# An RWKV-6 attention with an erf-softplus MLP on one Trainium2 core: the seven-product projection applied to four more units, with activations in chunks through PSUM

## The chip, the cores and the metric

The kernel runs on one core of a Trainium2 chip. Its engines are TensorE (PE, matrix products), VectorE (DVE), ScalarE (ACT), GpSimd (POOL) and SyncE (SP, here only a queue of DMAs). PSUM is the memory that the products are written to. The kernel's tiles in it are `pp0`, `pp1` and `y` of 1024 fp32 elements for each partition and two buffers `m` of 512, and no others.

The metric is the time of one execution in microseconds, and lower is better. A profile is one execution recorded by the hardware profiler, with the start and length of every instruction.

## The reference

All data are fp32. Attention has 4 batches, 8 heads, 768 tokens and head dimension 48. Its output, as 3072 rows of 384, goes through a two-layer MLP of width 2048.

```python
for t in range(S):
    cur = einsum('bhd,bhe->bhde', u * k[t], v[t])
    y[t] = einsum('bhd,bhde->bhe', r[t], state + cur)
    state = w[t][..., None] * state + einsum('bhd,bhe->bhde', k[t], v[t])
x = y as (3072, 384)
h = x @ w_in
sp = maximum(h, 0) + log1p(exp(-abs(h)))      # softplus
out = (h * erf(sp)) @ w_out
```

## The kernel before

**Units and steps.** The work is cut into 12 units (`n_steps`): a unit is 128 tokens of two batches, so 256 rows (`UNIT`) of the MLP. A unit passes through three stages. In step s the kernel attends unit s, computes the hidden layer of unit s-1 and projects unit s-3. All engines follow an order written out by hand: inside `tc.manual_schedule` (line 940) every engine executes its instructions in the order in which the program issues them, and dependencies through tiles become waits.

**Attention** works on chunks of 128 tokens. The masked products inside a chunk are built by levels: at level n, `level_products` (line 443) multiplies keys and queries that were decayed up to blocks of half that size, `take_level` (line 459) puts the result in `own`, and `scale` (line 257) multiplies keys and queries by the decay totals of that level (`tot_sb`, made on POOL at line 315). From step 4 on (`DIRECT`), the lowest levels are instead computed straight on DVE and POOL in `prepare` (lines 343 to 428): products of rows at distance 1 to 4 on DVE, 5 to 15 on POOL (lines 374 to 381), reduced on DVE into `sums` (line 367), sent through DRAM (`by_blocks`, `by_tokens`) and spread into `own` (line 423). `prepare(s + 1)` is a generator that step s advances with `next(following)`, so its parts lie among the step's other work.

**A late step** (`attend_late`, line 571, s > 4) issues in this order: `from_own` of the unit before (first group, into `y`), `fence` (a small DVE read of `y`), level five products, their scaling and masking, `from_own` (second group) and `through_state` of the unit before (lines 476 and 499), whose result ACT copies from `y` to `xT`. Then come the preparation of unit s+1, the scaling of `kT` by `spread` (line 595), and the places 0 to 4 at which MLP work is issued; between places 1 and 2 are level six, `spread_blocks`, the state product (`state_part`, line 530) and the sum `middle` (line 613), and between places 2 and 3 the new state (line 621). `products` (line 131) alternates between `pp0` and `pp1`.

**The MLP** comes in pieces: `piece` (line 893) advances a generator by one. A hidden piece (`hidden`, line 724) makes 512 elements for each partition in an `m` buffer, which ACT copies to `h`; eight pieces make a unit, in two tiles `h` of 8 by 256. After each tile `activate` queues three stages in `later`: softplus and Erf on ACT over the whole tile (2048 elements), and a multiplication on DVE in two halves. `advance` (line 875) issues these stages, up to one ACT activation at a time. Softplus and Erf each need an ACT table load, since they alternate.

**Projection.** Units 0 to 7 use `project` (line 767), eight pieces of four matmuls of 384 columns (each fp32 matmul is two instructions in the profile). Units 8 to 11 use `project_fast` (line 829): the matrices of activations and weights are cut into quarters and multiplied with seven quarter products in place of eight, after Winograd's form of Strassen's method. It needs four sums of weights (`mix_weights`, line 796, issued in steps 8 to 10) and four sums of activation quarters (`blend`, line 812, each 1024 elements), and two sums at the output (lines 864 and 868). `FAST = 8` is the first unit that uses it. The pieces of a step are ordered by strings in `in_order` (line 903), in which A is `advance`, P a projection piece and H a hidden piece.

Of the kernel before, what the change touches and what calls it, by code (L numbers as in the profile page):

```python
# [11 lines left out]
FP32 = mybir.dt.float32  # L12
I32 = mybir.dt.int32
# [4 lines left out]
P = 128  # L18
FAST = 8
EP = 64  # L20
HC = 64
# [40 lines left out]
def kernel(  # L62
# [34 lines left out]
    hid = ctx.enter_context(tc.tile_pool(name="hid", bufs=4))  # L97
    act = ctx.enter_context(tc.tile_pool(name="act", bufs=2))
    wide = ctx.enter_context(tc.tile_pool(name="wide", bufs=4))
# [25 lines left out]
    ND = DM // NJ  # L125
    mixed = const.tile([P, 3, FG, ND], FP32, name="mixed")
    y = ps_y.tile([P, NE, NJ, NP // 2, C], FP32, name="y")

# [138 lines left out]
    def prepare(s):  # L267
# [132 lines left out]
        for level in range(1, near_log(s)):  # L400
            scale(s, level)
        yield
        if near == NEAR:
# [15 lines left out]
        scale(s, near_log(s))  # L419
        if s > FAST:  # L420
            next(mixing)
        nb = HC // NEAR
# [6 lines left out]
        )  # L429
        if s == FAST + 3:  # L430
            next(mixing)

# [66 lines left out]
    def through_state(s, xT):  # L499

        c, in_t, _, _, S, _, _ = parts_of(s)
        for h, state in enumerate((S, middle)):
            if not (c or h):
                continue
            t = slice(h * HC, (h + 1) * HC)
            for j in range(NJ):
                for q in range(0, NP, 2):
                    for e in range(NE):
                        for p in (q + e, q + 1 - e):
                            n = j * NP + p  # L510
                            nc.tensor.matmul(  # L511
                                y[at(e, p), e, j, p // 2, t],
                                lhsT=state[rows(e), n, :], rhs=in_t[rows(e), 0, n, t],
                                start=False, stop=True, skip_group_check=True,
                            )

        y3 = att.tile([P, UNIT], FP32, name="y3", bufs=1)
        nc.scalar.copy(y3[:].rearrange("p (j t) -> p j t", j=NJ), y[:, 1, :, 1])
        for j in range(NJ):
            nc.scalar.copy(xT[:, 0:2, j * C : (j + 1) * C], y[:, 0, j])  # L520
        nc.scalar.copy(xT[:, 2, :].rearrange("p (j t) -> p j t", j=NJ), y[:, 1, :, 0])
        for kk in range(KT):
            n = D // KT
            for e, queue in enumerate((nc.sync, nc.scalar)):
                queue.dma_start(
                    out=xT[e * EP + D : (e + 1) * EP, kk, :],
                    in_=y3[e * EP + kk * n : e * EP + (kk + 1) * n, :],
                )
# [41 lines left out]

    def attend_late(s, place):

# [3 lines left out]
        if before:  # L576
            from_own(before, ready[before][0], 1)
            fence()
        pp = products([P, NE, JP, HC])
        level_products(pp, RK, LOG - 1)  # L580
# [10 lines left out]
        next(following, None)  # L591
        if s == FAST + 3:
            blend(FAST, gated[FAST])
        kT = kTs[s]
# [3 lines left out]
        )  # L598
        place(0)
        next(following, None)  # L600
        place(1)

        pp = products([P, NE, JP, HC])
        level_products(pp, RK, LOG)
        if s + 1 < n_steps:
            spread_blocks(s + 1, pp)
        take_level(own, pp, LOG)
        ps = products([P, NC, JP, HC])
        ps = [ps[:, h] for h in range(NC)]
        state_part(s, kT, ps)  # L610
        scale(s, LOG)
        for e in range(NE):
            nc.vector.tensor_add(middle[rows(e)], faded[0][rows(e)], ps[0][rows(e), :, :D])
        place(2)
        next(following, None)
        if s < n_steps - SPC:
# [3 lines left out]
            for e in range(NE):  # L620
                nc.vector.tensor_add(S_next[rows(e)], faded[1][rows(e)], ps[1][rows(e), :, :D])
        place(3)
        for _ in following:
            pass
        place(4)

# [94 lines left out]

    later = []

    def hidden(of, xT, gs, cut):


        def activate(h):
# [3 lines left out]
            def softplus():  # L731
                held.append(act.tile([P, FG, UNIT], FP32, name="sp"))
                nc.scalar.activation(held[0][:], h[:], AF.Softplus)  # L733

            def erf():
                nc.scalar.activation(held[0][:], held[0][:], AF.Erf)  # L736

# [4 lines left out]
            later.extend([(softplus, True), (erf, True), (multiply, False)])  # L742
            if of > FAST and len(gs) == NG:
                later.append((lambda: blend(of, gs), False))

        for g in range(NG):
            h = hid.tile([P, FG, UNIT], FP32, name="h")
            gs.append(h)
            for f in range(0, FG, FT):
# [12 lines left out]
                nc.scalar.copy(h[:, f : f + FT, :], ps[:])  # L762
                if f == FG - FT:
                    activate(h)
# [44 lines left out]

    blends = {}  # L810

    def blend(of, gs):

        if of % 2:
            rooms = [wide.tile([P, 2, DM, 2], I32, name="words", bufs=3) for _ in range(3)]
            rooms = [x[:].rearrange("p x n two -> p (x n two)").bitcast(FP32) for x in rooms]
        else:
            two = att.tile([P, 2, JP, C], FP32, name="rk1", bufs=1)
            one = ins.tile([P, JP, C], FP32, name="w")
            rooms = [x.rearrange("p n t -> p (n t)") for x in (two[:, 0], two[:, 1], one[:])]  # L820
        s1, s2, s4 = (x[:, : FG * C].rearrange("p (f t) -> p f t", t=C) for x in rooms)
        (a11, a21), (a12, a22) = [[g[:, :, j * C : (j + 1) * C] for j in range(NJ)] for g in gs]
        nc.vector.tensor_add(s1, a21, a22)
        nc.vector.tensor_sub(s2, s1, a11)
        nc.vector.tensor_sub(s4, a12, s2)
        nc.vector.tensor_sub(a21, a11, a21)
        blends[of] = s1, s2, a21, s4

# [74 lines left out]
    def in_order(s, k):  # L903


        order = ("APPPAPP", "APPP", "HH", "AHHH", "AHHH", "PPAPP")
        if s == DIRECT:
            order = ("APPP", "APPP", "APPHH", "AHHH", "AHHH")
        if s >= FAST + 3:
            order = ("PAPPPAP", "PAP", "HH", "AHHH", "AHHH", "PPPAP")  # L910
        for what in order[k]:
# [4 lines left out]
            else:  # L916
                piece(hids, s - 1)


    CONVERT = (  # L920
# [19 lines left out]
    with tc.manual_schedule(  # L940
# [20 lines left out]
        for s in range(n_steps):  # L961
# [8 lines left out]
            def place(n):  # L970
                if n == (LOG - 1 if s <= DIRECT else 2) and DIRECT - 1 <= s < n_steps - 2:
                    load_rows(s + 2)
                for due in {(3, 4): (5,), (4, 3): (6,), (4, 5): (7,)}.get((s, n), ()):
                    load_w(due)
                if s > DIRECT and n == 2 and s + 3 < n_steps:
                    load_w(s + 3)
                if s >= DIRECT:
# [13 lines left out]
                beside(s, next(places))  # L991

            if s > DIRECT:
                attend_late(s, place)
                continue
# [8 lines left out]
            if s + 2 < n_steps:  # L1004
                load_step(s + 2)
                if s + 2 == DIRECT:
                    load_rows(s + 2)
        s = n_steps - 1
        from_own(s, ready[s][0], 1)
        fence()  # L1010
        advance()
        piece(projs, s - 2)
        from_own(s, ready[s][0], 0)
        through_state(s, xTs[s])
        in_order(s + 1, 5)
        for k in range(1, 15):
            in_order(s + 1 + k // 5, k % 5)

# [95 lines left out]
```

## Time and profile before

| | us |
|---|---|
| median of 3 runs (607.51 to 608.27) | 607.88 |
| profiled execution | 607.66 |
| its span | 605.9 |
| PE busy | 592.9 |
| PE weight loads busy (beside PE) | 470.8 |
| DVE busy | 439.5 |
| ACT busy | 294.3 |
| POOL busy | 296.1 |

Steps 5 to 11 begin at 202.9, 247.4, 295.2, 341.5, 387.8, 434.05 and 480.85 us of the span, and what follows step 11 at 524.57. Busy time (us) in each of these stretches:

| step | length | PE | DVE | ACT | POOL |
|---|---|---|---|---|---|
| 5 | 44.50 | 44.50 | 38.85 | 20.20 | 31.88 |
| 6 | 47.80 | 46.54 | 38.92 | 20.80 | 33.55 |
| 7 | 46.30 | 46.30 | 38.93 | 20.79 | 32.00 |
| 8 | 46.30 | 46.30 | 40.67 | 20.80 | 32.19 |
| 9 | 46.25 | 46.25 | 40.64 | 20.79 | 33.39 |
| 10 | 46.80 | 46.58 | 41.17 | 20.79 | 26.55 |
| 11 | 43.72 | 43.72 | 20.02 | 20.82 | 0 |
| after | 81.33 | 77.80 | 22.39 | 31.94 | 0 |

A share of busy time alone does not say what a change is worth: an engine's waits, and the order in which its instructions stand, decide when its results come. The chain of the profile follows the work back from the last instruction, at each step to what released it. The granted clock of PE was full (1.00) in every one of these stretches.

### The profile page before, as it was taken

Reading aid. Unit: us, or ns where it says so; the run is one execution under the profiler, and the core shown is the slowest. Engines: PE = TensorE matmul, PEld = TensorE weight load, DVE = VectorE, ACT = ScalarE, POOL = GpSimd, SP = SyncE. Lnnn points to the kernel's source line nnn. Section 1 sums busy time; section 2 is a strip of 40 time slices with the busy share of each in tenths; the row PEclk is TensorE's granted clock in tenths of the full one; section 3 lists DMA queues with packets and bytes.
Section 4 is the critical chain, followed back from the end, with each engine's and each line's share of the span. In section 5 each row is a group of like instructions: output and inputs, shape, how many; then the busy total and the mean of one; then the engine's idle time right before and its main releaser. Section 6 shows DMA issues by size and latency. Waiting matters only on the chain.

```text
span 605.9 us, 16024 instructions
## 1 busy us (share of the span) xinstructions
PE 592.9 (98%) x7050; PEld 470.8 (78%) x7050; DVE 439.5 (73%) x487; ACT 294.3 (49%) x378; POOL 296.1 (49%) x295
## 2 busy tenths in 40 slices
PE   8889999999999999999999999999999999999997
PEld 7668787678668768658758858858857898898997
DVE  5688597895995897897697798898798756105141
ACT  2648887635536533442552462462462463652440
POOL 4349175602397489489369569659659200000000
PEclk9999999999999999999999999999999999999999
DMA  8376471441333405325325334334321300000000
GB/s 322 117 279 222 156 257 58 202 147 13 138 78 132 131 26 176 68 84 190 48 103 157 76 109 154 75 112 120 71 102 56 70 8 28 1 21 13 1 28 26
DMA packets 51373, 63.29 MB, mean 104 GB/s; under 512 B 34920, under 2 KB 40296, under 8 KB 49896
## 3 DMA queue, kind: packets, MB, share of 16 engines
q1 hardware_dynamic: 50152, 61.68, 32.0%
q8 instruction: 55, 0.90, 0.6%
q10 hardware_dynamic: 1152, 0.59, 0.4%
q14 instruction: 14, 0.11, 0.1%
HBM read 52.39 MB, written 8.69 MB: 101 GB/s over the span
## 4 chain that ended last, share of the span: by engine, by line
PE 85%; DVE 7%; issue 2%; POOL 2%; ACT 2%; DMA 1%; SPq 0%; DVEq 0%; POOLq 0%; ACTq 0%
PE m L753 38%; PE m L782 25%; PE m L844 12%; PE pp L451 5%; DVE in L263 2%; PE y L485 2%; PE y L511 1%; PE pp L537 1%; POOL w_in_sb L232 1%; DMA in<-in_rkw 1%; DVE w_in_sb L228 1%; PE pp L682 1%; DVE sums L367 1%; DVE pp L220 1%; DVE own L463 1%
## 5 line engine op out<-in xcount | busy, mean ns | idle before, releaser
L753 PE MATMUL m<-xT,w_in_sb 128*128 128x256 f32 x1152 | 257.3, 382 | 2.4 <-DVE w_in_sb L228 1.2
L753 PEld LDWEIGHTS m<-xT,w_in_sb 128*128 128x128 f32 x1152 | 216.1, 190 | 34.6 <-issue 3.6
L782 PE MATMUL m<-w_out_sb,h 128*128 128x384 f32 x512 | 168.6, 489 | 0.0
L782 PEld LDWEIGHTS m<-w_out_sb,h 128*128 128x128 f32 x512 | 96.2, 190 | 65.3
L762 ACT COPY h<-m 128x512 f32<-128x512 f32 x96 | 56.0, 583 | 132.1 <-PE m L753 131.9
L263 DVE TENSOR_TENSOR in<-in,tot_sb 128x1024 f32<-128x1024 f32 (+1 forms) x60 | 84.4, 1414 | 18.6 <-PE pp L451 16.8
L740 DVE TENSOR_TENSOR h<-h,sp 128x1024 f32<-128x1024 f32 x48 | 74.6, 1594 | 23.8 <-ACT sp L736 23.6
L381 POOL TENSOR_TENSOR words<-words,rest 128x528 f32<-128x528 f32 (+10 forms) x77 | 85.6, 1111 | 6.0
L377 POOL TENSOR_TENSOR rk<-words 128x528 f32<-128x528 f32 (+3 forms) x28 | 44.5, 1590 | 78.7 <-DVE sums L367 68.3
L315 POOL TENSOR_TENSOR tot_sb<-tot_sb 128x256 f32<-128x256 f32 (+4 forms) x60 | 57.6, 960 | 4.5
L451 PEld LDWEIGHTS pp<-in 48*64 48x64 f32 (+1 forms) x2368 | 33.8, 125 | 16.1 <-issue 8.3
L733 ACT ACTIVATE sp<-h 128x2048 f32<-128x2048 f32 x24 | 45.9, 1911 | 0.3
L736 ACT ACTIVATE sp<-sp 128x2048 f32<-128x2048 f32 x24 | 45.9, 1911 | 0.3
L367 DVE TENSOR_REDUCE sums<-words 128x6 f32<-128x288 f32 (+8 forms) x66 | 29.2, 469 | 19.3 <-POOL words L377 19.0
L451 PE MATMUL pp<-in 48*64 48x64 f32 (+1 forms) x2368 | 38.4, 212 | 3.8 <-issue 1.6
L791 ACT COPY o<-m 128x384 f32<-128x384 f32 x16 | 7.7, 478 | 65.6 <-PE m L782 65.6
L736 ACT ACT_TABLE_LOAD x24 | 30.8, 1283 | 13.2 <-issue 12.9
L377 POOL TENSOR_TENSOR words<-words 128x336 f32<-128x336 f32 (+6 forms) x49 | 35.1, 715 | 3.8
L367 DVE TENSOR_REDUCE sums<-rk 128x14 f32<-128x672 f32 (+9 forms) x54 | 34.8, 703 | 0.2
L733 ACT ACT_TABLE_LOAD x24 | 30.8, 1283 | 3.1 <-issue 2.8
L381 DVE TENSOR_TENSOR words<-words,rest 128x576 f32<-128x576 f32 (+8 forms) x34 | 27.9, 820 | 1.2
L232 POOL TENSOR_TENSOR w_out_sb<-w_out_sb,rest 128x768 int32<-128x768 int32 x8 | 17.8, 2222 | 17.8 <-DVE w_out_sb L228 17.7
(110 smaller groups left out, 625.3 us busy)
## 6 DMA issues: line engine op xcount, KB each, us to landing
in<-in_rkw SPq DMA_DIRECT2D x11, 1024.0 KB, 5.0
words<-in_moe_w_in SPq DMA_DIRECT2D x8, 768.0 KB, 5.5
words<-in_moe_w_out SPq DMA_DIRECT2D x8, 768.0 KB, 4.1
words<-in_rk_rows SPq DMA_DIRECT2D x8, 768.0 KB, 6.9
w<-in_rkw SPq DMA_DIRECT2D x11, 512.0 KB, 8.5
v<-in_v SPq DMA_DIRECT2D x12, 384.0 KB, 5.8
out<-o SPq DMA_DIRECT2D x24, 192.0 KB, 1.9
rest<-in_w_rows SPq DMA_DIRECT2D x8, 384.0 KB, 7.1
```

Of the source, the lines that this page charges most:

```text
L263: nc.vector.tensor_mul(halves, halves, view(tots[level - 1], 0, [[1, n], [2, nb], [0, half]]))
L315: nc.gpsimd.tensor_mul(new, pair[:, :, 0], pair[:, :, 1])
L367: nc.vector.tensor_reduce(out=view(sums[:], n, [[near * (NEAR + 1), NEAR // near], [NEAR + 1, near - n]]), in_=terms[n], axis=mybir.AxisLi ...
L377: engine.tensor_mul(terms[n], r[:, :, n:], k[:, :, : near - n])
L381: engine.tensor_mul(k[:, :, :m], k[:, :, :m], w[:, :, n : n + m])
L451: nc.tensor.matmul(pp[s0 : s0 + m, e, n, :m], lhsT=rk[rows(e), 1, n, s0 : s0 + m], rhs=rk[rows(e), 0, n, t0 : t0 + m], start=True, stop=True,)
L733: nc.scalar.activation(held[0][:], h[:], AF.Softplus)
L736: nc.scalar.activation(held[0][:], held[0][:], AF.Erf)
L740: nc.vector.tensor_mul(h[:, part], h[:, part], held[0][:, part])
L753: nc.tensor.matmul(ps[:, ff, :], lhsT=w_in_sb[:, g * FG + f + ff, kk * P : (kk + 1) * P], rhs=xT[:, kk, :], start=kk == 0, stop=kk == KT - 1,)
L782: nc.tensor.matmul(ps[j][:], lhsT=gs[g][:, f, j * C : (j + 1) * C], rhs=w_out_sb[:, g * FG + f, :], start=g + f == 0, stop=g == NG - 1 and ...
L844: nc.tensor.matmul(to, lhsT=a[:, f], rhs=b[:, f], start=start and f == 0, stop=f == FG - 1, skip_group_check=True,)
```

## The change

- `FAST` becomes 4, so units 4 to 11 use the seven-product projection. The sums of weights move to steps 5 (three) and 6 (one).
- From unit 4 on, softplus and Erf work on chunks of 1024 elements, four a unit in place of two tiles of 2048. Softplus writes into a fixed SBUF tile `room`, and Erf writes into PSUM, alternately into `y` and `pp1`, which serve as two "lanes". DVE multiplies `h` by the lane.
- For the sums of activation quarters, ACT copies three quarters (22, 11 and 12) into the lanes, so each of the four sums reads one operand from PSUM. The four sums S1 to S4 of unit s-2 are spread over step s; their results go into `room`.
- In late steps all level and state products use `pp0`, since `pp1` is a lane. Level six with its copies and scaling goes between the fifth and the sixth projection piece, and the state product behind the last one.
- The three `xT` DMAs that ACT issued in a late step go to SP. The loads of rows and of `w` for later steps are issued after the state sum `middle` and the first blends, in place of before it, and the first three scalings of `prepare` become three separate parts.
- The order of late steps is written as strings: s is softplus of a chunk, ey and ep Erf into `y` or `pp1`, m the multiplication, k22y the copy of quarter 22 into `y`, S and a number a sum, F the next part of `prepare`, T a sum of weights.

```diff
-FAST = 8
+FAST = 4
...
+    room = const.tile([P, 4, FG * C], FP32, name="room")
...
         for level in range(1, near_log(s)):
             scale(s, level)
-        yield
+            if s > DIRECT + 1:
+                yield
+        if s <= DIRECT + 1:
+            yield
...
-        if s > FAST:
-            next(mixing)
...
-            for e, queue in enumerate((nc.sync, nc.scalar)):
+            for e, queue in enumerate((nc.sync, nc.sync if s > DIRECT else nc.scalar)):
...
-        place(0)
-        next(following, None)
-        place(1)
-
-        pp = products([P, NE, JP, HC])
+        run(0, following)
+
+        pp = products([P, NE, JP, HC], 0)
         level_products(pp, RK, LOG)
         if s + 1 < n_steps:
             spread_blocks(s + 1, pp)
         take_level(own, pp, LOG)
-        ps = products([P, NC, JP, HC])
+        scale(s, LOG)
+        run(1, following)
+        ps = products([P, NC, JP, HC], 0)
         ps = [ps[:, h] for h in range(NC)]
         state_part(s, kT, ps)
-        scale(s, LOG)
+        run(2, following)
...
+    def lane(kind):
+
+        if kind == "y":
+            return y[:].rearrange("p e j q t -> p (e j q t)")
+        return products([P, NE * JP * HC], 1)[:]
+
+    def softplus_chunk():
+        nc.scalar.activation(sp_room, chunks[0], AF.Softplus)
+
+    def erf_chunk(kind):
+        at = lane(kind).rearrange("p (f t) -> p f t", t=UNIT)
+        nc.scalar.activation(at, sp_room, AF.Erf)
+        started.append((chunks.pop(0), at))
+
+    def multiply_chunk():
+        h, at = started.pop(0)
+        nc.vector.tensor_mul(h, h, at)
...
+    def to_lane(of, what, kind):
+        lanes[what] = lane(kind).rearrange("p (f t) -> p f t", t=C)
+        nc.scalar.copy(lanes[what], quarter(of, what))
+
+    def blend(of, *parts):
...
+        for part in parts or (1, 2, 4, 3):
+            if part == 1:
+                nc.vector.tensor_add(s1, s3, a["22"])
+            elif part == 2:
+                nc.vector.tensor_sub(s2, s1, a["11"])
+            elif part == 3:
+                nc.vector.tensor_sub(s3, a["11"], s3)
+            else:
+                nc.vector.tensor_sub(s4, a["12"], s2)
...
+    LATE = {
+        DIRECT + 1: (
+            "A P P P A P P", "F F F A P P P", "", "H H F", "A s H ey m H H F T T s H ep m H H T"
+        ),
+        DIRECT + 2: (
+            "s P P ey m P s P ep m P", "k22y P P F P k11p T F F", "S1", "S2 S3 H k12y H F",
+            "S4 s H ey m H H F s H ep m H H",
+        ),
+        n_steps - 1: (
+            "s P ey m P s P ep m P P", "P P", "S", "H H", "s H ey m H H s H ep m H H"
+        ),
+    }
+    USUAL = (
+        "s P ey m P s P ep m P P", "k22y P F P k11p F F", "S1", "S2 S3 H k12y H F",
+        "S4 s H ey m H H F s H ep m H H",
+    )
...
+            def run(n, following):
+                if n == 3 and s < n_steps - 2:
+                    load_rows(s + 2)
+                if n == 3 and s + 3 < n_steps:
+                    load_w(s + 3)
+                run_late(s, LATE.get(s, USUAL)[n], following)
```

`run_late` takes the tokens of a string one by one and calls the functions above.

## The prediction

> **What bounds the kernel now.** I read the busy shares first, then the chain that ended last, then single steps of the timeline. Columns of the chain are start, length (us), engine, tile, line, count.
>
> ```profile
> PE 592.9 (98%) x7050; PEld 470.8 (78%) x7050; DVE 439.5 (73%) x487; ACT 294.3 (49%) x378; POOL 296.1 (49%) x295
> ```
> ```profile
> 295.21 0.59 PE y L485 x32
> 295.80 0.93 PE pp L451 x64
> 296.74 0.45 PE y L485 x32
> 297.18 0.90 PE y L511 x64
> 298.08 20.84 PE m L782 x64
> 318.92 0.69 PE pp L451 x50
> 319.85 0.72 PE pp L537 x62
> 320.57 20.92 PE m L753 x96
> 341.49 0.59 PE y L485 x32
> ...
> 483.72 18.40 PE m L844 x112
> ```
>
> From 203 us on, the chain is TensorE alone. One step (here step 7, from its first `from_own` at 295.21 to the next at 341.49, 46.3 us) is a list of PE work: 0.59 + 0.93 + 0.45 + 0.90, a plain projection of 20.84, level six and block spreading 0.93, state 0.72, hidden layer 20.92. The last line shows a seven-product projection: 18.40. So each of the four units moved to it can give PE 2.44 us, 9.8 in all, but only while no other engine is as long as PE. VectorE (DVE) decides that. In the same step (columns start, length, engine, line, operation, tiles, count):
>
> ```profile
> 295.87 0.17 DVE L494 COPY seen<-y 128x16 f32<-128x16 f32 x1 [3.78 <-PE y L485]
> ...
> 311.03 1.72 DVE L595 TENSOR_TENSOR kT<-kT,spread 128x768 f32<-128x768 f32 x1
> ...
> 312.67 4.25 DVE L740 TENSOR_TENSOR h<-h,sp 128x1024 f32<-128x1024 f32 x2
> ...
> 313.89 1.96 POOL L377 TENSOR_TENSOR rk<-words 128x432 f32<-128x432 f32 x1
> ...
> 316.85 2.12 DVE L263 TENSOR_TENSOR in<-in,w 128x1024 f32<-128x1024 f32 x1
> ...
> 319.07 5.08 DVE L263 TENSOR_TENSOR in<-in,tot_sb 128x1024 f32<-128x1024 f32 x3
> ...
> 324.07 1.11 DVE L613 TENSOR_TENSOR middle<-faded,pp 48x384 f32<-48x384 f32 x2
> ...
> 332.00 0.20 DVE L367 TENSOR_REDUCE sums<-words 128x1 f32<-128x48 f32 x1 [0.57 <-POOL words L377]
> ...
> 333.15 1.12 DVE L621 TENSOR_TENSOR s<-faded,pp 48x384 f32<-48x384 f32 x2 [0.95 <-POOL faded L617]
> ...
> 338.34 1.31 DVE L423 TENSOR_TENSOR own<-block_sb,by_tokens 128x1024 f32<-128x1024 f32 x1
> ```
> ```profile
> 295.20:341.50 46.30, 46.30 (x489) 34.61 (x492) 38.93 (x44) 20.79 (x25) 32.00 (x33) 1.00 0.39 112
> ```
>
> The reader should see three things. DVE works without a pause from 296.81 to 325 and is only then held up by GpSimd (POOL). Its operations with both inputs in SBUF are stretched while POOL runs: the multiply of `h` takes 2.13 us here (4.25 for two), though the rows' smallest is 1.18; `middle` (an input in PSUM) takes 0.55 for 384 elements with POOL beside it, as at the end of the kernel with POOL idle. And its spare time is small: 3.78 us idle before the fence at 295.87, and 2.50, 0.76, 0.76 and 1.38 before the next four.
>
> **The change part by part.** Times below are offsets from a step's first `from_own` unless they have a date. The sum is made on the profiled execution: 607.66 us, of which 605.9 is span and 1.76 lies around it; the median of the runs is 607.88, 0.04% more.
>
> *PE.* Units 4 to 7 lose 2.44 each, in steps 7 to 10. A usual step becomes: first piece at 2.87, five pieces of 18.40/7 = 2.63 to 16.0, level six and spreading to 16.9, two pieces to 22.2, state to 22.9, then eight hidden pieces of 20.92/8 = 2.615, the fifth ending at 36.0, the eighth at 43.85. Using one bank pair for levels and state costs nothing here: two pieces (5.3 us) stand between level six and the state product, and the copies that free the pair are 0.23 + 1.16 on ACT; without those pieces it would be 1.4.
>
> *Activations.* Eight of 1024 elements replace four of 2048. The rows give 0.89 for 768 and 1.91 for 2048, so by interpolation 1.09 each, 8.7 in place of 7.6. Table loads double, from four of 1.28 to eight: +5.1. Three copies to PSUM: 0.58 for 512 and 0.80 for 768 make 1.0 for 1024, +3.0. The projection copies are 0.32 + 0.48 + 0.32 in place of 0.96. ACT goes from 20.8 to about 30 of its step and stays off the bound by busy time. The trace shows no drain around a load: an Erf ends at 304.41, the load runs 304.43 to 305.71, the next activation starts at 305.73.
> The Trainium skill ("ScalarE: Activation LUTs", What ACT_TABLE_LOAD costs) says otherwise: about 1.38 us of drain comes on top of 1.283 for every switch. By that rule the four added loads would be 10.6 us of ACT a step, not 5.1, which is an estimate from the page, and ACT would be at about 41 of 49. The row decides, and the sum goes by it.
>
> *Multiplies of `h`.* Four a step, with Erf's result now in PSUM. No row has a 1024-element multiply of this kind beside POOL. Ends: 1.22 (line 670, 1024 elements, one input in PSUM) and 2.13 (both inputs in SBUF, POOL beside). I take 1.22, because `middle` is not stretched beside POOL.
>
> *Blends.* Units 4 to 7 get four 1024-element sums each on DVE, in steps 6 to 9; unit 8's moves into step 10 (before, it stood in step 11). Each has an input in PSUM: 1.22 to 2.13 by the same rows, 1.22 taken. Two sums at the output of each fast unit, 0.55 each (line 864), replace ACT copies.
>
> *Weight sums.* Four operations of 1.75 (1.84 beside POOL) leave steps 8 to 10, where DVE's idle time hid most of them, and go to step 5 (three) and step 6 (one).
>
> *DMAs.* Three `xT` DMAs a step leave ACT's queue for SP's: three took SP 1.79, so six are 3.6, and `load_step` behind them starts 1.8 later. The hidden layer needs `xT` 20 us later and the next step needs its inputs 27 us later, so 0; without that cover it would be 1.8 a step. Row and `w` loads go behind the state sum, ahead of the `k_blocks` and `by_blocks` issues: three issues of 0.44, or 1.3, and the masks built from `by_tokens` are needed at the step's end: 0.
>
> *The new wait.* This is where I put the loss. PSUM bank pair `y` now carries, in one step, Erf, a copy of quarter 22, a copy of quarter 12, and Erf again. The second Erf (chunk 0 of the next unit) must wait until the fourth sum S4 has read quarter 12. In ACT's order it stands ahead of the fourth hidden piece's copy, and PE has two `m` banks, so hidden piece six waits for that copy. When does DVE end S4? Up to the end of line 595 nothing changes: 312.67, offset 17.46. Then two multiplies 2.44 to 19.9; the four scalings of rows 316.85 and 319.07, 7.22 with gaps, and the two output sums 1.1, to 28.2; S1 to 29.4; `middle` 1.14 to 30.6; S2 and S3 to 33.0; eleven reductions 4.5 to 37.5 (POOL, freed from the stretched multiplies, has by my count delivered its last term by about 36); the state sum 1.15 to 38.7; S4 to 39.9. Erf 1.09 to 41.0 (load done while waiting), copy 0.58 to 41.6. PE ended piece five at 36.0 and stands 5.6 us. Three more pieces, 7.85, end the step at 49.4 in place of 46.3. The next fence then waits for PE again, so every usual step has this length.
>
> *Step 5.* DVE ended its queue at 247.03 before. Two more multiplies (2.44) and three weight sums (5.25) make it 254.7, so the fence, and PE behind it, run at 254.7 in place of 248.07.
>
> *The sum.* Step 6 from the fence at 254.9: scaling and mask 1.8, the line 384 to 595 stretch 14.1, then as above plus one weight sum 1.8 and without the output sums: S4 ends at 294.0, the copy at 295.7, and step 7 begins at 303.5 in place of 295.2 (+8.3; PE alone would be there at 299.7). Steps 7, 8 and 9 at 49.4 end at 451.7, step 10 (no state sum) at 48.3 ends at 500.0, before 480.85: +19.2. Steps 11 and the end have no POOL work and the same PE work as before (43.7 and 81.3): 0. So 607.66 + 19.2 = 626.9, and 627 for the median.
>
> **Bounds.** With no stretching left, line 595 is 0.95 and the four scalings 4.35 (three of 1.22 and 0.69): 3.64 less in each of five steps, 18.2, so 609. With multiplies and sums stretched after all, five operations ahead of S4 gain 0.91 each in five steps: +22.7, so 650. If the wait also holds back the table load, 1.28 in five steps: +6.4, 633.
>
> **Rivals.**
> *A: PE stays the bound, faster.* DVE would have to end S4 by 36.0 - 1.7 = 34.3, 5.6 sooner than I count. Then step 7 starts at 299.7, four steps of 43.85 end at 475.1, 5.75 ahead: 602. It breaks even where S4 is 19.2/5 = 3.84 sooner, about all the stretching there is. For it: POOL has less to collide with; against it: everything up to 17.46 is unchanged and the rest adds up row by row.
> *B: lighter stretching, still slower.* Scalings fall behind POOL's long terms and pay half or less: between 609 and 617.
> *C: copies and Erf in PSUM stretch DVE all the same:* 640 to 650, the upper bound. Against it: `middle`.
>
> **How the numbers follow.** Forecast (617 to 640, DVE's chain through S4): 0.66. B: 0.13. A: 0.12. C: 0.09. The likeliest gives 627. The range leaves out A and the upper part of C: 609 to 643. Within 0.2%, about what a measurement of this kernel can tell from no change, 606.7 to 609.1, lies only the lower edge of B and the upper edge of A: 0.04. Faster 0.11, slower 0.85.
>
> **What would show it.** Right: PE idle or its `m` matmuls of line 753 stopped for about 5 us once in each of steps 6 to 10, released by an ACT copy of `h`, ACT's Erf waiting for DVE's fourth sum, hidden layers of about 26.5 in place of 20.92; projections of units 4 to 7 of 18.4; `h` multiplies near 1.2; a fence near 254.7. Wrong: a whole chain of PE pieces at 43.9 a step, S4 ending before offset 34, or multiplies and sums near 2.1.

## The result, and the profile after

The median of the changed kernel is 638.23 us (637.26 to 640.65) against 607.82 (607.51 to 608.27): 5% longer, with a ratio of the means of 1.0506 and a 95% interval of 1.0474 to 1.0537. Its profiled execution took 637.57 us with a span of 635.5, so +29.9 us on the profiled execution before; the forecast was +19.2.

From the page of the changed kernel: busy times, the granted clock in 40 slices, the chain by engine, the two groups of `h` multiplies.

```profile
PE 595.5 (94%) x7242; PEld 501.3 (79%) x7242; DVE 441.2 (69%) x511; ACT 352.5 (55%) x461; POOL 272.7 (43%) x295
...
PEclk9999999999999999898999999899899999999999
...
PE 51%; DVE 21%; POOL 18%; issue 5%; ACT 4%; DMA 1%; SPq 0%; POOLq 0%; DVEq 0%; ACTq 0%
...
L735 DVE TENSOR_TENSOR h<-h,pp 128x1024 f32<-128x1024 f32 x16 | 19.4, 1215 | 48.9 <-ACT pp L730 48.9
L735 DVE TENSOR_TENSOR h<-h,y 128x1024 f32<-128x1024 f32 x16 | 19.5, 1217 | 42.2 <-ACT y L730 42.2
```

PE's busy time grew by only 2.6 us and DVE's by 1.7, while the span grew by 29.6. So time went into waiting: the chain that was PE for 85% is now PE for half of it, and DVE, POOL and ACT hold most of the rest. The clock row has slices at 8 where it had none before, and what PE does at a lower clock counts as busy for longer. The multiplies run at 1.22.

The waits of the changed kernel (engine and tile, what it waited for: total us, times, longest):

```profile
ACT L730 <- DVE room L862: 25.2, 5, 6.6
...
PE m L770 <- ACT h L779: 18.2, 5, 5.2
...
PE y L484 <- DVE seen L493: 5.9, 1, 5.9
...
PE y L510 <- issue: 2.5, 2, 1.4
...
PE m L879 <- DVE o L899: 1.6, 1, 1.6
```

Erf's line (L730) waited five times for the fourth sum (L862), and five times TensorE's hidden pieces (L770) waited for the copy to `h` (L779): one chain, in steps 6 to 10. PE's five waits are 1.95, 5.19, 3.96, 4.01 and 3.10 us. Step 7 shows the chain (start, length, engine, line, operation, idle before it; the step begins at 306.77):

```profile
324.29 1.21 DVE L735 TENSOR_TENSOR h<-h,y 128x1024 f32<-128x1024 f32 x1
...
327.62 1.66 DVE L263 TENSOR_TENSOR in<-in,w 128x1024 f32<-128x1024 f32 x1
...
333.09 1.21 DVE L856 TENSOR_TENSOR room<-h,y 128x1024 f32<-128x1024 f32 x1
...
335.36 1.22 DVE L858 TENSOR_TENSOR room<-room,pp 128x1024 f32<-128x1024 f32 x1
...
343.20 1.12 DVE L617 TENSOR_TENSOR s<-faded,pp 48x384 f32<-48x384 f32 x2 [0.96 <-POOL faded L613]
...
344.35 1.23 DVE L862 TENSOR_TENSOR room<-y,room 128x1024 f32<-128x1024 f32 x1
...
345.65 1.28 ACT L730 ACT_TABLE_LOAD   x1 [6.60 <-DVE room L862]
...
346.95 1.03 ACT L730 ACTIVATE y<-room 128x1024 f32<-128x1024 f32 x1
347.91 1.06 ACT L779 COPY h<-m 128x512 f32<-128x512 f32 x2
...
348.54 9.69 PE L770 MATMUL m<-xT,w_in_sb 128*128 128x256 f32 x36 [5.19 <-ACT h L779]
...
358.16 0.67 PE L484 MATMUL y<-own,v 64*48 64x64 f32 x32
```

S4 ends at 345.58 (offset 38.8). Only then does ACT begin the table load, then Erf, then the copy that frees the `m` buffer; PE goes on at 348.54 after 5.19 us. The last three hidden pieces then take 9.69 us; the same 36 records took 8.04 where the clock was full. The stretches of the changed kernel (length, busy us of PE, weight loads, DVE, ACT, POOL, granted clock, DMA share, GB/s): the first two are just before and after 352 us, the others steps 7 and 10.

```profile
348.50:352.00 3.50, 3.46 (x8) 2.83 (x9) 3.00 (x3) 2.81 (x3) 0.00 (x0) 0.51 0.34 62
352.00:356.00 4.00, 4.00 (x20) 3.51 (x19) 0.00 (x0) 2.88 (x4) 0.00 (x0) 1.00 0.00 0
```
```profile
306.80:358.20 51.40, 46.21 (x537) 41.85 (x536) 39.94 (x50) 29.23 (x37) 26.77 (x33) 0.97 0.32 101
...
460.90:508.40 47.50, 44.40 (x505) 40.62 (x504) 38.98 (x48) 29.22 (x37) 22.67 (x23) 1.00 0.26 73
```

For 3.5 us after the wait the granted clock is 0.51, and then it is full. In step 10 the wait is shorter and the clock stays full. In step 6 the wait is the shortest of the five, and yet the same pieces take 9.72:

```profile
500.40 8.04 PE L770 MATMUL m<-xT,w_in_sb 128*128 128x256 f32 x36 [3.10 <-ACT h L779]
...
297.12 9.72 PE L770 MATMUL m<-xT,w_in_sb 128*128 128x256 f32 x36 [1.95 <-ACT h L779]
```

So the length of a wait does not decide it. The granted clock of this trace changes only at the ends of stretches of 3.41 us that lie on a fixed grid. The same columns for such stretches around both waits:

```profile
293.90:297.31 3.41, 1.46 (x7) 0.96 (x7) 0.98 (x2) 3.07 (x4) 2.17 (x8) 1.00 0.83 117
297.31:300.72 3.41, 3.41 (x9) 2.70 (x9) 2.76 (x3) 2.58 (x3) 0.00 (x0) 0.50 0.28 37
...
495.28:498.70 3.42, 2.03 (x10) 1.44 (x8) 1.70 (x4) 1.19 (x1) 1.75 (x4) 1.00 0.41 150
498.70:502.11 3.41, 1.71 (x8) 1.53 (x9) 2.24 (x2) 3.38 (x5) 0.00 (x0) 1.00 0.35 41
502.11:505.52 3.41, 3.41 (x18) 3.00 (x17) 1.34 (x2) 3.27 (x5) 0.00 (x0) 1.00 0.78 119
```

The 1.95 us of step 6 lie in one stretch, PE is busy for 1.46 us of it, and the next stretch is at 0.50. The 3.10 us of step 10 are divided between two stretches with 2.03 and 1.71 us of work, and both are followed by full clock. The rest of this trace fits: stretches with PE busy for 1.46 us or less are followed by slow clock, those with 1.68 or more are not. The other traces draw no sharp line there, since stretches with 1.5 to 2.1 us of work were followed by either.

A second wait stands once, in step 6: PE waits 5.86 us for the fence. Two stretches of the grid, from 252.94 to 259.77, are at 0.50 there.

```profile
255.78 1.10 PE L484 MATMUL y<-own,v 64*48 64x64 f32 x32 [5.86 <-DVE seen L493]
```

Where the 29.6 us of span lie, by the starts of the steps: 1.0 before step 6; 10.65 in step 6 (58.45 in place of 47.8); 5.1, 5.15 and 4.9 in steps 7 to 9; 0.7 in step 10 (47.5 in place of 46.8); 0.2 in step 11; 1.85 after it.

### The profile page after: what moved, and what is told of

It is laid out like the page before. It is cut to its first block, busy times and chain, and to the rows that moved or that the text cites. A ratio compares the mean times of both kernels' runs of the same rounds, so it can differ in the third digit from the quotient of the medians.

```text
span 635.5 us, 16524 instructions
## 1 busy us (share of the span) xinstructions
PE 595.5 (94%) x7242; PEld 501.3 (79%) x7242; DVE 441.2 (69%) x511; ACT 352.5 (55%) x461; POOL 272.7 (43%) x295
## 4 chain that ended last, share of the span: by engine, by line
PE 51%; DVE 21%; POOL 18%; issue 5%; ACT 4%; DMA 1%; SPq 0%; POOLq 0%; DVEq 0%; ACTq 0%
PE m L770 25%; PE m L879 13%; POOL words L381 10%; PE pp L450 5%; PE m L802 4%; POOL words L377 4%; POOL rk L377 3%; DVE words L381 3%; DVE sums L367 3%; DVE in L263 3%; DVE rk L377 2%; PE y L484 1%; ACT L730 1%; DVE own L462 1%; DVE room L862 1%
## 5 line engine op out<-in xcount | busy, mean ns | idle before, releaser
L770 PE MATMUL m<-xT,w_in_sb 128*128 128x256 f32 x1152 | 264.7, 388 | 20.4 <-ACT h L779 18.2
L770 PEld LDWEIGHTS m<-xT,w_in_sb 128*128 128x128 f32 x1152 | 220.0, 194 | 56.0 <-ACT h L779 20.2
L779 ACT COPY h<-m 128x512 f32<-128x512 f32 x96 | 55.3, 581 | 99.6 <-PE m L770 99.3
L802 PE MATMUL m<-w_out_sb,h 128*128 128x384 f32 x256 | 86.1, 493 | 0.0
L735 DVE TENSOR_TENSOR h<-h,pp 128x1024 f32<-128x1024 f32 x16 | 19.4, 1215 | 48.9 <-ACT pp L730 48.9
L735 DVE TENSOR_TENSOR h<-h,y 128x1024 f32<-128x1024 f32 x16 | 19.5, 1217 | 42.2 <-ACT y L730 42.2
L879 PE MATMUL m<-w_out_sb,h 128*128 128x192 f32 x256 | 45.0, 329 | 1.6 <-DVE o L899 1.6
L879 PE MATMUL m<-mixed,h 128*128 128x192 f32 x256 | 44.8, 328 | 0.0
L879 PEld LDWEIGHTS m<-mixed,h 128*128 128x128 f32 x256 | 41.7, 190 | 0.3
L315 POOL TENSOR_TENSOR tot_sb<-tot_sb 128x256 f32<-128x256 f32 (+4 forms) x60 | 37.4, 623 | 4.5
L879 PE MATMUL m<-w_out_sb,room 128*128 128x192 f32 x224 | 38.7, 326 | 0.0
L879 PEld LDWEIGHTS m<-w_out_sb,room 128*128 128x128 f32 x224 | 36.8, 190 | 0.0
```

The source lines that it names most:

```text
L315: nc.gpsimd.tensor_mul(new, pair[:, :, 0], pair[:, :, 1])
L735: nc.vector.tensor_mul(h, h, at)
L770: nc.tensor.matmul(ps[:, ff, :], lhsT=w_in_sb[:, g * FG + f + ff, kk * P : (kk + 1) * P], rhs=xT[:, kk, :], start=kk == 0, stop=kk == KT - 1,)
L802: nc.tensor.matmul(ps[j][:], lhsT=gs[g][:, f, j * C : (j + 1) * C], rhs=w_out_sb[:, g * FG + f, :], start=g + f == 0, stop=g == NG - 1 and ...
L879: nc.tensor.matmul(to, lhsT=a[:, f], rhs=b[:, f], start=start and f == 0, stop=f == FG - 1, skip_group_check=True,)
```

## The experiments

All of them are made on the changed kernel. The median of the kernel before beside them was 607.70 to 607.88.

### Exchange the lanes of the two Erfs

My theory: PE stands because the first Erf behind S4 uses the lane `y`, which S4 still reads. A rival reading: ACT, which has four more table loads and three more copies a step, is itself too long late in the step, and the lane is beside the point.

```diff
-            "S4 s H ey m H H F s H ep m H H",
+            "S4 s H ep m H H F s H ey m H H",
```
(in the strings of the usual steps and of step 6)

> The two Erf chunks at the end of steps 6 to 10 change lanes: the first writes pp1, the second y. All work stays. Theory (the first Erf waits for the sum S4 that still reads lane y, and PE waits for the copy queued behind that Erf on ACT): pp1 is free since S3, some 8 us earlier, so the 5.2 us of standing PE before hidden piece six and the slow clock behind it go. Steps 7 to 9 fall from 51.4 to 44 to 45, step 10 from 47.5 to 44, step 6 by about 4: 638.2 becomes 608 to 614. Rival (VectorE's queue as a whole is the bound, whichever lane): it then holds PE elsewhere, steps stay above 48, and the time above 622. If the second Erf holds the step's end instead, steps of 46 to 47 and about 618.

Measured: 614.30 us (613.53 to 619.45), ratio 1.0125 [1.0083, 1.0167], 23.9 us below the changed kernel. The same stretch of step 7 in this kernel:

```profile
325.52 20.99 PE L770 MATMUL m<-xT,w_in_sb 128*128 128x256 f32 x96
...
334.46 1.28 ACT L730 ACT_TABLE_LOAD   x1
...
335.75 1.03 ACT L730 ACTIVATE pp<-room 128x1024 f32<-128x1024 f32 x1
...
339.67 1.23 DVE L862 TENSOR_TENSOR room<-y,room 128x1024 f32<-128x1024 f32 x1
...
342.23 1.28 ACT L730 ACT_TABLE_LOAD   x1
```

The hidden pieces run as one group of 20.99 us. The table load starts at once behind a copy, 5 us before S4, and S4 ends at the same offset as before, 38.8, with nobody waiting for it. ACT does the same work, so that rival falls. So does the recorded one, DVE's queue as a whole: S4 is as late as before, and the time is far below 622. The steps are 44.3, 46.0, 45.4, 45.1 and 45.6 us from step 7 on; the 5.9 us ahead of step 6 remain.

### No copy of quarter 12

The other way to take S4 off the lane: the sum reads quarter 12 from SBUF.

```diff
-"S2 S3 H k12y H F"
+"S2 S3 H H F"
```

> The changed kernel with one edit: the copy of quarter 12 into lane y is left out and S4 reads it from SBUF. Another way of taking the same wait away: lane y is then free since S1. Theory (the wait on S4's read of lane y is the cause, not the lane that Erf writes): as with changed lanes, 612 to 617, S4 itself 1.2 to 2.1 us. Rival (changing lanes helped by where the second multiply lands): above 625.

Measured: 612.48 (611.97 to 612.93), 1.0074 [1.0059, 1.0090]. Steps 7 to 11 take 44.3, 45.8, 45.7, 44.2 and 43.9, PE's wait for the copy of `h` is gone, and the 5.9 us before step 6 stay. S4 takes 1.28 on average with both inputs in SBUF in place of 1.22. So this one copy, which saves DVE less than 0.1 us each time, together with an Erf on the same lane makes the wait that costs 25 us.

### Weight sums earlier

```diff
         def place(n):
+            for _ in range(3 if (s, n) == (DIRECT - 1, LOG) else 0):
+                next(mixing)
...
-"A s H ey m H H F T T s H ep m H H T"
+"A s H ey m H H F s H ep m H H"
```

> The three sums of weights of step 5 move to step 3, in front of the state sum, where VectorE stood 5.8 us in the profile before. Theory: the fence of step 6 comes 5.3 us sooner, PE no longer stands 5.9 us in front of it nor runs slowly behind it, and step 6 keeps its later wait: 638.2 becomes 630 to 633. Rival (the fence is late for another reason, or VectorE's lag only moves): within 2 us of 638.

Measured: 635.46 (630.36 to 637.62), 1.0442 [1.0385, 1.0499]. The wait before step 6 is gone (second `from_own` at 251.04 in place of 255.78) and step 7 starts 6.3 us earlier; but its span ends only 2.8 us earlier, and the median missed the expected 630 to 633. PE's pieces behind the wait in steps 9 and 10 of this kernel:

```profile
445.28 11.09 PE L770 MATMUL m<-xT,w_in_sb 128*128 128x256 f32 x36 [4.03 <-ACT h L779]
...
495.92 9.68 PE L770 MATMUL m<-xT,w_in_sb 128*128 128x256 f32 x36 [3.15 <-ACT h L779]
```

They took 11.09 and 9.68 us, where the changed kernel needed 9.42 and 8.04 for the same, after waits of the same length (4.03 and 3.15 here, 4.01 and 3.10 there). These two make 3.3 of the 3.5 us that were given back. The grid of the clock separates them from the changed kernel: here nearly all of step 10's wait lies in one stretch (PE busy for 0.31 us from 492.46 to 495.87) and the next one is at 0.50, and in step 9 two stretches in a row, from 444.67 to 451.49, are at 0.50, the second behind one in which PE was busy for 2.80 us, all at the slow clock. That the runs scatter over 7 us fits waits that lie differently on the grid, but is not shown to come from it.

### Extra products in the wait

If the slow pieces come from PE's standing still, products that keep it working should make them fast. Six products of 384 columns into `pp0` go between the fifth and the sixth hidden piece; their results are not used.

```diff
-"S4 s H ey m H H F s H ep m H H"
+"S4 s H ey m H H W F s H ep m H H"
...
+            elif what == "W":
+                idle = products([P, NE * JP * HC], 0)
+                for i in range(6):
+                    nc.tensor.matmul(idle[:, :DM], lhsT=ident[:], rhs=w_in_sb[:, i], ...)
```

> Every wait stays; PE gets six extra products (about 0.65 us each, 3.9 us) into pp0 between hidden pieces five and six of steps 6 to 10, while it would stand. Their results are not used. Theory that the slow 1.8 us behind each stand is the granted clock falling because PE stands: pieces six to eight take 7.9 in place of 9.4 to 9.7, 1.8 less in each of four steps: 638.2 becomes 630 to 632. Rival (the slow pieces have another cause, such as waits for ACT copies): 638 or, where the extra work overruns the stand, up to 642.

Measured: 635.91 (634.69 to 636.19), 1.0458 [1.0443, 1.0474]. Step 7 of this kernel on PE:

```profile
310.46 0.32 PE L510 MATMUL y<-in,middle 48*48 48x64 f32 x4 [1.40 <-issue]
310.70 4.55 PE L879 MATMUL m<-w_out_sb,h 128*128 128x192 f32 x16
...
345.83 4.05 PE L984 MATMUL pp<-w_in_sb,ident 128*128 128x384 f32 x12
349.91 8.04 PE L770 MATMUL m<-xT,w_in_sb 128*128 128x256 f32 x36
```

The three pieces are back at 8.04, and the granted clock stays at 1.00 behind the wait, so standing still is what slows them. The median moved only 2.3 us, though, where 6 to 8 were expected. Steps 8 and 9 became 1.4 and 1.5 shorter, as expected; step 7 did not, since a gap of 1.40 us without any cause in the records ("issue") and a first projection piece of 4.55 in place of 2.97 stand ahead of S4, which ended at offset 40.8 in place of 38.8. That piece is slow clock too: 0.50 from 310.87 to 314.28, behind a stretch with the gap in it, in which PE was busy for 2.01 of 3.41 us. Steps 6 and 10 were 0.5 longer, which was not followed up.

### Both mends

```diff
-"S4 s H ey m H H F s H ep m H H"
+"S4 s H ep m H H F s H ey m H H"
...
+            for _ in range(3 if (s, n) == (DIRECT - 1, LOG) else 0):
+                next(mixing)
```

> Both edits: lanes changed, three weight sums in step 3. Theory: the gains add, since they lie in different steps but for step 6: 600 to 606, below the kernel before (607.8). Rival (VectorE's total work bounds the steps): above 615.

Measured: 607.40 (606.80 to 609.64), 0.9998 [0.9989, 1.0008]: no change from the kernel before, where I had expected 2 to 8 us less. The hidden pieces and the fence do not wait any more, and yet the steps take 44.4 to 45.8. Steps 7 to 10 together are 5.4 us shorter than in the kernel before; what stands ahead of step 6, step 11 and the end are 4.1 longer. What is left on PE:

```profile
PE y L510 <- issue: 4.2, 4, 1.3
...
PE pp L450 <- issue: 1.7, 2, 1.3
PE m L879 <- DVE o L899: 1.6, 1, 1.6
```

These are gaps of up to 1.3 us in the burst of small products at a step's start, with no event that ends them. Steps 8, 9 and 11 have one and take 45.4 to 45.8; steps 7 and 10 have none and take 44.4 and 44.6.

### A projection piece inside that burst

If the gaps come from the density of the small products, a projection piece between `take_level` and the second `from_own` should remove them.

```diff
             take_level(own, pp, LOG - 1)
         if before:
+            run_late(s, "P")
             from_own(before, ready[before][0], 0)
```
(on top of both mends, with one P less in the strings)

> On top of lanes changed and early weight sums (607.4): in each late step the first projection piece goes between level five's masking and the second from_own group, so the run of small products at a step's start (about 390 PE instructions in 2.9 us) is cut in two with 2.6 us of long products between. Theory (PE there waits for its own instructions, which arrive in blocks of 256: 57 packets of 16.3 KB on the instruction queue for some 14,500 PE instructions): the 5.9 us of PE idle put down to issue shrink to under 2, and 607.4 becomes 603 to 604.5. Rival (these gaps are waits for VectorE's fence that the profile misnames, or instruction arrival is slow whatever stands there): 606 to 608.

Measured: 607.83 (607.29 to 610.43), 1.0003 [0.9987, 1.0019]. The gaps of L510 are gone, as the theory said, but the time isn't:

```profile
PE m L880 <- ACT o L891: 3.8, 5, 0.8
```

Now PE waits in each step for a copy that frees an `m` buffer of the projection, since ACT has a softplus and an Erf with their loads ahead of it. One piece earlier, the copies of the projection are earlier against ACT's list, and the list was not moved.

### The end of the kernel

```diff
-        run_late(s + 1, "s P ey m P s P P ep m P S P P")
+        run_late(s + 1, "s P ey m P s ep m P P S P P P")
```
(on top of both mends)

> On top of lanes changed and early weight sums: in the last-but-one projection the Erf into pp1 and its multiply come two pieces earlier and the four sums S one piece earlier, so that VectorE's output sums are not queued behind them. Theory: the 1.6 to 1.9 us that PE stands there go, 607.4 becomes 605.4 to 605.9. Rival (another wait takes its place at the last Erf): 607 to 608.

Measured: 606.15 (605.13 to 608.11), 0.9970 [0.9955, 0.9985]. The wait of the last unit's first piece for an output sum is gone, and the time is just above the expected 605.4 to 605.9. With the split burst as well:

> All four edits together: lanes changed, early weight sums, cut run of small products, tail order. Theory: gains add to 601.3 to 603, below the kernel before (607.75) by about 1%. Rival (VectorE's 44 us of queue in a step of 43.9 takes over as the bound): 605 or more.

Measured: 606.83 (606.12 to 609.05), 0.9980 [0.9964, 0.9995], where 601 to 603 were expected; the same wait for ACT's copy, 4.1 us in all, stays. The time lies in the range of the recorded rival, DVE's queue as the bound, but the next run, with DVE's work the same, is below that range.

### The first softplus ahead of the burst

ACT's list moved along: the first softplus of a step is issued with the early projection piece.

```diff
-            run_late(s, "P")
+            run_late(s, "s P")
...
-"s P ey m P s P ep m P"
+"P ey m P s P ep m P"
```
(on top of both mends, the split burst and the end; the other strings likewise)

> All four edits, and the first softplus of each late step issued together with the early projection piece, before the xT copies. In the run with the cut burst ACT's two activations held the third projection copy, and PE stood 0.8 us before the fifth piece in each of five steps. Theory: with softplus some 4 us earlier that wait goes, steps of 45.6 become 44.2 to 44.8, and the time 601 to 603.5. Rival (VectorE's queue is by now as long as PE's list, and the steps stay at 45.5): 605 to 607.

Measured: 601.63 us (601.59 to 602.54), ratio 0.9899 [0.9884, 0.9915]. That is 1% below the kernel before and 36.6 us below the changed one. Its page and its waits:

```profile
PE 586.6 (98%) x7242; PEld 494.8 (82%) x7242; DVE 440.6 (73%) x511; ACT 353.2 (59%) x461; POOL 275.8 (46%) x295
...
PEclk9999999999999999999999999999999999999999
```
```profile
PE pp L450 <- issue: 0.9, 1, 0.9
...
PE m L880 <- ACT o L891: 0.3, 1, 0.3
```

Steps 7 to 11 take 44.76, 44.53, 44.52, 45.1 and 44.3. This is the time that the prediction gave to rival A, 602, but not by A's condition: S4 ends at offset 39.0 in step 7, as late as ever, and nobody waits for it.

### Chunks without the four fast units

What does the change cost without its gain? `FAST = 8` again, chunks from unit 4 on, early weight sums, no copies and sums for units 4 to 7. Step 10 keeps the sums, for unit 8, with the lanes exchanged.

```diff
-FAST = 4
+FAST = 8
...
-                if of >= FAST:
+                if of >= DIRECT:
...
-        "s P ey m P s P ep m P P", "k22y P F P k11p F F", "S1", "S2 S3 H k12y H F",
-        "S4 s H ey m H H F s H ep m H H",
+        "s P P ey m P s P ep m P", "P P F P F F", "", "H H F",
+        "s H ey m H H F s H ep m H H",
```

> The chunked activations through PSUM from unit 4 on, but the seven-product projection only from unit 8 on as before; units 4 to 7 use the plain projection without sums and copies, three weight sums in step 3, one in step 10, whose two last Erf chunks use the changed lanes. So no Erf waits for a sum. Theory (chunks and their eight table loads cost nothing on the path; the loss was the wait on lane y): 608 to 611, the 1.9 us of the tail included. Rival (chunks, table loads or pp0 alone for the levels cost by themselves): above 615.

Measured: 612.15 (611.18 to 613.87), 1.0065 [1.0045, 1.0085]. The start of step 6 is 1.6 us late, step 6 takes 48.4 in place of 47.8, the next steps 46.6 in place of 46.3, and the end 83.2 in place of 81.3. So chunks alone cost about 4 us and not 30 (611 was the most expected); the 25 us need S4 and Erf on one lane. Part of the start is not theirs: in this execution the granted clock was 0.94 on average in the first 31 us, and the executions at full clock took 611.2 to 611.5.

### The fastest version without any copies to PSUM

```diff
-"k22y P P F P k11p T F F", "S1", "S2 S3 H k12y H F",
+"P P F P T F F", "S1", "S2 S3 H H F",
```
(step 6; in the usual steps in the same way)

> As the run with all edits and early softplus, without the three copies to PSUM: the sums S1 to S4 read SBUF alone. Theory (a sum with both inputs in SBUF is stretched by POOL, 1.22 becoming 1.5 to 2.1, as the multiplies of h in the kernel before): S1 to S3 take 0.3 to 0.9 more each, VectorE has about 1.5 us spare in a step, so 0 to 2 us more in each of five steps: 602 to 611. Rival (the copies buy nothing): equal to the run with copies within 1, or faster by ACT's freed 3 us.

Measured: 614.35 (612.16 to 616.91), 1.0103 [1.0081, 1.0125], 12.7 us above the version with copies; I had expected 602 to 611 us in all. The sums of this kernel (times, then busy us and mean ns), and what PE waits for:

```profile
L861 DVE TENSOR_TENSOR h<-h 128x1024 f32<-128x1024 f32 x8 | 12.4, 1552 | 0.0
...
L857 DVE TENSOR_TENSOR room<-h 128x1024 f32<-128x1024 f32 x7 | 12.0, 1715 | 0.0
...
L859 DVE TENSOR_TENSOR room<-room,h 128x1024 f32<-128x1024 f32 x7 | 10.5, 1494 | 0.2
```
```profile
PE y L484 <- DVE h L736: 8.7, 5, 2.5
```

S1 to S3 take 1.49 to 1.72 us on average in place of the 1.21 to 1.22 with one operand in PSUM, though the averages hold two or three at the end of the kernel at 1.22, where POOL is idle (S4, 1.24, is not stretched). POOL pays too: its 295 instructions take 298.1 us in place of 275.8. DVE's list ends later, and PE waits for DVE's last multiply, from which `from_own` takes the lane `y` over. Not all of the 12.7 us is this wait: the start is 1.1 later, and in two steps the clock is at 0.50 for 3.4 us.

## Why the prediction was right

The sign, the place and the mechanism were as forecast; the time, 638.2, lies in the range and in the likeliest case's own, and 11 us above its middle. That it is still inside is in part luck. The range was made for stretched operations and for the table load; the slow clock, which took some 7 us of it, was not in it. And S4 came 0.8 to 2.1 us sooner than the sum had it in steps 7 to 10; without that some 5 us more would have come on top, as an estimate from these offsets.

**The new wait.** Right, and shown from two sides: with the lanes exchanged, or without the copy of quarter 12, PE's wait for the copy of `h` disappears and 24 to 26 us with it. S4 ended at offset 38.8 where the sum gave 39.9: the four scalings met less of POOL (5.6 us of busy time in place of 7.2), so S1 started at 26.3 and not at 28.2, and the state sum gave 0.9 of this back, since it waited for POOL's `faded` (0.96), a wait that the trace of before shows and the sum left out. So a part of rival B, lighter stretching, was there as well. In step 6, S4 ended at 294.15 (forecast 294.0).

**"Load done while waiting".** Wrong. The taken value was 0, and the bound of 1.28 in each of five steps is what happened: every one of the five table loads starts after S4. With S4 1.1 sooner PE went on at offset 41.77 in step 7, where the sum had the copy's end at 41.6, and in step 6 the copy ended at 297.1 against 295.7. The drain that the Trainium skill adds to a load ("ScalarE: Activation LUTs", What ACT_TABLE_LOAD costs) is in no line here: the load above starts at 345.65, 0.07 behind S4, and runs for 1.28, and Erf starts at 346.95.

**"Three more pieces, 7.85".** This is the term that failed most. They took 9.4 to 9.7 in steps 6 to 9, 1.6 to 1.9 more each, since the granted clock fell to half for 3.4 us after PE had stood still, for 1.95 us in step 6 and 4 to 5.2 in steps 7 to 9. With that the hidden layer of step 7 took 28.0, where about 26.5 was forecast. The extra products in the wait gave 8.04 back, so the cause is shown. The trace of before had no such wait late in a step, and I priced the pieces at full clock. The Trainium skill has the rule ("TensorE: Matmul & The Clock Gate", Why this matters for your kernels): no idle gaps over about 3 us between bursts, or the clock halves. The runs agree in step 7, with 5.19 and 0.51, but not everywhere: 3.10 left the clock full in step 10, 3.15 did not in the kernel with early weight sums (9.68), and 1.95 did not in step 6. What separates them is how much PE worked in the 3.41 us stretch before, as shown above.

**Step 5.** Right: the fence stood at 255.56 (forecast 254.7), and moving the three weight sums removes the wait and starts step 7 6.3 us earlier.

**The sum.** Forecast and profiled time differ by 10.7. Step 6 has 3.3 of it (1.4 for the table load and S4, 1.9 for the clock), steps 7 to 9 have 2.0, 2.05 and 1.8 (1.6 to 1.85 of it clock, the rest a later end of the wait; in steps 8 and 9 "issue" gaps of 1.4 and 1.1 stand ahead, and PE's wait was about 4 in place of 5.2), step 10 has -0.8, step 11 0.2, what follows it 1.85, and the time outside the span 0.3.

**The end, priced at 0.** It cost 1.85, of which 1.58 is a projection piece of the last unit waiting for an output sum that stands behind four sums on DVE:

```profile
611.80 1.22 DVE L860 TENSOR_TENSOR h<-h 128x1024 f32<-128x1024 f32 x1
612.94 0.55 DVE L899 TENSOR_TENSOR o<-o,m 128x384 f32<-128x384 f32 x1
...
613.54 2.87 PE L879 MATMUL m<-w_out_sb,h 128*128 128x192 f32 x16 [1.58 <-DVE o L899]
```

With Erf, its multiply and the sums moved forward the end has no such wait. I had compared PE's work in this stretch and not the order of DVE's.

**The multiplies and sums at 1.22.** Right (1.215 and 1.217, sums 1.21 to 1.23), which excludes rival C. That the operand in PSUM does it is shown for the sums: without the copies three of the four take 1.49 to 1.72. For the multiplies it was not tried apart. The Trainium skill states this ("SBUF — State Buffer", Who interferes with whom): an operation of DVE with two SBUF inputs contends with GpSimd's reads, one with a single SBUF input does not, outside the 2-port modes.

**Rival A** was a matter of order, not of work: with the same instructions in another order PE is the bound again, and the time is 601.6. A's condition, S4 by offset 34.3, was not needed and not met. Not all is settled. Steps of 44.5 there are 0.7 above the sum's 43.85, although PE has no idle time in step 8 (44.53 busy of 44.53); in step 7, by the starts of its pieces, the projection takes 18.8 in place of 18.4, and the hidden layer and the small products the rest, and why was not followed up. What makes the "issue" gaps is open; those at L510 are gone where a projection piece splits the burst.

## What to carry to other kernels

When a buffer gets a second user, write down for each engine in order who waits behind the one that must now wait: here one ACT instruction waiting for DVE's last sum held a copy behind it, and the copy held TensorE. Price a wait of TensorE with the slow clock that follows it, and a waiting activation with its table load, which waits with it. A change that loses by 5% may still hold a gain: the exchange of two letters gave 24 us back, and four more changes of order made it 1% faster than the kernel before.

## What was not expected of the hardware

- The granted clock fell to 0.50 for 3.41 us, or twice that, after waits of TensorE of 1.95 to 5.9 us, but not always: 3.10 left it full, 1.95 and 3.15 did not. In the changed kernel it went by the stretch of 3.41 us before, on a fixed grid: slow after 1.46 us of work or less in it, full after 1.68 or more.
- A wait of an activation was found on the table load ahead of it in all five steps (6.60 us before the load in step 7, none between load and Erf).
- In the bursts of small products TensorE stood for up to 1.6 us with no event in the trace that ends the gap; the instruction queue moved 57 packets (55 before). The kernel before has such a gap too (1.26 us in step 6). A piece of large products in the middle of the burst removed those at L510. Whether instruction supply is the cause was not tried.
- Without the copies to PSUM, the same sums S1 to S3 at the same places in the order took 1.49 to 1.72 us in place of 1.22, POOL's same instructions 298.1 in place of 275.8 in all, and the kernel 12.7 us more, though the copies are three ACT operations a step.
